# Waiting for the output's landing on TensorE instead of SyncE in a decode kernel

## The chip, the cores and the metric

The kernel runs on one core of a Trainium2 chip. The metric is device time in microseconds of one execution of the program; lower is better. The time quoted for a kernel is a median over several executions. A profile of one further execution goes with it; its own time is stated beside its span, because the span is only the time from the first to the last instruction of the kernel and the execution's time is a little longer.

## The reference

A decode step for four sequences (B = 4, one new token each, D = 576). Two branches read the same normalised input and are added to the residual:

```python
x = A_x
xn = _layernorm(x)
return x + A(xn) + B(xn)

# A: attention over a cache
q = (x @ wq).reshape(4, 1, 32, 128)          # 32 query heads, 16 kv heads
k, v = last 2048 rows of k_cache, v_cache    # each 4 x 16 x 2048 x 128 bf16
o = softmax(q k^T * 128**-0.5) v
return o.reshape(4, 1, 4096) @ wo            # wo: 4096 x 576

# B: an MLP pair with a shift in time
h  = gelu(layernorm(x) @ w1)                 # 576 x 576
x1 = x + shift(h) @ w2                       # 576 x 576
return x1 + gelu(layernorm(x1) @ w3) @ w4    # 576 x 4608, 4608 x 576
```

Nearly all bytes are the keys and values: 2 x 33.6 MB in bf16. The output is 4 x 576 values in bf16, 4.6 KB.

## The kernel before

The program is written as lists of operations, one list for each engine (`prog["pe"]`, `"pe2"`, `"pe3"`, `"dve"`, `"act"`, `"pool"`, `"sp"`). `add` appends an operation with the events it waits for, the event it signals and a key; `add_dma` does so for a DMA (its issue is L199). Each list is sorted by key and then written out by `emit_program`, which puts the waits ahead of the operation (L640). The order of an engine's work is therefore the order of the keys. TensorE's three lists are written with two loops between them: `pe`, then the loop over the keys, then `pe2`, then the loop over the values, then `pe3`.

The stages, in order of time:

- The small first part: layer norms on VectorE and ScalarE, the products with wq, w1, w2 and w3 on TensorE (lists `pe`).
- Keys: 16 chunks of 2 MB are loaded into a ring of 4 slots by DMAs that SyncE issues. TensorE transposes each chunk block by block (L485), VectorE and ScalarE move the blocks from PSUM to SBUF (L469, L468), TensorE forms the scores (L492).
- Softmax, and a transposition of the probabilities by matmuls (L514, list `pe2`).
- Values: 8 chunks of 4 MB through 4 slots. VectorE spreads the probabilities over heads (L545), TensorE multiplies (L553).
- The end (list `pe3`): the attention output is folded and transposed, then h2 @ w4 and o @ wo are accumulated into the same two PSUM tiles, `ACC[0]` and `ACC[1]` (one for each half of the 576 columns; both by L392). wo comes in five pieces of 13, 10, 5, 3 and 1 of its 32 rows for a partition, so that TensorE has little left to do when the last piece lands. ScalarE copies one half to `out_sb` (L608), VectorE the other (L609), and ScalarE issues the DMA of `out_sb` to the output (its key is 10000, the last of its list).

SyncE's list holds all loads except x, in the order of their keys, each behind the event that frees its slot. Its last operation, with key 10001, is a bare wait: it holds SyncE until the semaphore of the output's DMA has its full count (L301). Nothing stands behind it in SyncE's list. The events "PV..." that release the last loads are those of the values' products, so SyncE has issued its last load long before the end.

The last operations of `pe3` are the products with the last piece of wo, written for h = 1 and then for h = 0 with the events `AOl1` and `AOl0`, which L609 and L608 wait for.

Of the kernel before, what the change touches and what calls it, by code (L numbers as in the profile page):

```python
# [37 lines left out]
def bass_parallel_sum__sliding_block_cached__mixer_s_mlp__decode_kernel(  # L38
# [31 lines left out]
    with ExitStack() as ctx:  # L70
# [100 lines left out]
        S = {}  # L171
# [16 lines left out]
        def add(engine, emit, waits=(), sig=None, key=0.0, inc=None):  # L188
            seqc[0] += 1
            prog[engine].append(Op(emit, waits, sig, key, seqc[0], inc))  # L190

        def add_dma(pairs, skey, waits=(), key=0.0, engine="sp"):
            if skey not in S:
                S[skey] = sem("s_" + "_".join(str(k) for k in (skey if isinstance(skey, tuple) else (skey,))))
            dma_count[skey] = dma_count.get(skey, 0) + 16 * len(pairs)

            def emit(e):
                for o_, i_ in pairs:
                    e.dma_start(o_, i_).then_inc(S[skey], 16)  # L199
            add(engine, emit, waits, None, key)  # L200
            return ("dma", skey, dma_count[skey])
# [96 lines left out]
            a += rc  # L298
        assert a == 32
        ev_o = add_dma([(o2, out_sb[:])], "out", ["fin1", "fin0"], 10000, engine="act")  # L300
        add("sp", lambda e: e.wait_ge(S[ev_o[1]], ev_o[2]), (), None, 10001)  # L301


        def ln_ops(idx, src, dst, first_waits, tag, k0):
# [346 lines left out]
        e = nc.tensor  # L651
# [66 lines left out]
```

## Time and profile before

| | |
|---|---|
| median of three executions | 214.03 us (213.77 to 214.03) |
| the profiled execution's own time | 213.93 us |
| its span, first to last instruction | 212.6 us |
| TensorE busy with matmuls | 172.5 us (81%) |
| VectorE busy | 111.9 us (53%) |
| ScalarE busy | 58.6 us (28%) |
| read from HBM | 88.49 MB, 416 GB/s over the span |
| mean granted clock of TensorE | 0.928 |

In the profile PE is TensorE (PEld its weight loads), DVE is VectorE, ACT is ScalarE, POOL is GpSimd and SP is SyncE. A q behind the name stands for the engine's sequencer, which does the waiting and issues the DMAs: "SPq L301" is an instruction of SyncE's sequencer from line 301. Waits of this kind are not counted as busy time.

A view of the profile prints what lies in the span. The trace itself also records the updates of all semaphores, each with its time, for some microseconds ahead of the span and behind it, where the runtime's own instructions run. These records are used below; they are quoted as a plain list, with times in us counted from the start of the span, as in all views.

### The profile page before, as it was taken

The numbers are of one execution on the slowest core, as the hardware profiler recorded it, in microseconds if no ns is written. First come the engines' busy times: TensorE is split into PE (matmuls) and PEld (weight loads), VectorE is DVE, ScalarE is ACT, GpSimd is POOL, SyncE is SP. The second block draws the span as 40 slices with busy tenths as digits, with TensorE's granted clock in tenths as the row PEclk, the third lists the DMA queues.
The fourth block names the chain that finished last, engine by engine and source line by source line (L and its number), as shares of the span: only waits on it lengthen the run. The fifth ranks groups of instructions, "written<-read, shape, count | busy, mean of one in ns | idle before, by whom it ended". The sixth has DMA issues, their size and how long they took to land.

```text
span 212.6 us, 4856 instructions
## 1 busy us (share of the span) xinstructions
PE 172.5 (81%) x2212; PEld 133.7 (63%) x2216; DVE 111.9 (53%) x168; ACT 58.6 (28%) x69; POOL 15.6 (7%) x38
## 2 busy tenths in 40 slices
PE   1456147999999999999996089999989598997495
PEld 0222014888878888887774048988868487883262
DVE  5433200477776777777764869995575444003000
ACT  2004001366665566666656520000000000000000
POOL 8991000000000000000000000000000000000000
PEclk9997855899999999999999589999999889999799
DMA  6999999999999999999999999999999999999993
GB/s 242 453 444 445 429 396 416 432 425 427 429 416 438 432 422 429 435 422 424 432 444 438 444 407 459 413 425 453 407 444 438 419 425 410 451 476 393 407 408 131
DMA packets 5066, 88.65 MB, mean 417 GB/s; under 512 B 568, under 2 KB 704, under 8 KB 1216
## 3 DMA queue, kind: packets, MB, share of 16 engines
q1 hardware_dynamic: 5040, 88.49, 97.7%
q8 instruction: 8, 0.13, 0.3%
q14 instruction: 2, 0.02, 0.0%
q10 hardware_dynamic: 16, 0.01, 0.0%
HBM read 88.49 MB, written 0.00 MB: 416 GB/s over the span
## 4 chain that ended last, share of the span: by engine, by line
DMA 47%; PE 45%; DVE 4%; SPq 1%; ACT 1%; issue 1%
PE ps L485 23%; DMA vring<-in_A_wo_dram 15%; DMA vring<-in_B_w_dram 13%; DMA vring<-in_A_v_cache_dram 12%; PE ps L553 11%; DMA kring<-in_A_k_cache_dram 7%; PE ps L492 6%; PE ps L430 2%; SPq L199 1%; DVE vring L520 1%; DVE rmax L498 1%; DVE ktb L545 1%; PE ps L514 1%; PE ps L347 1%; ACT ktb L468 0%
## 5 line engine op out<-in xcount | busy, mean ns | idle before, releaser
L469 DVE COPY ktb<-ps 128x1024 bf16<-128x1024 bf16 x80 | 53.8, 689 | 23.5 <-PE ps L485 23.4
L485 PEld LDWEIGHTS ps<-perm_bf,kring 128*128 128x128 bf16 x1024 | 58.2, 98 | 8.3 <-issue 7.6
L485 PE MATMUL ps<-perm_bf,kring 128*128 128x128 bf16 x1024 | 61.7, 220 | 0.2
L468 ACT ACTIVATE ktb<-ps 128x1024 bf16<-128x1024 bf16 x48 | 48.0, 1023 | 32.5 <-PE ps L485 32.1
L545 DVE TENSOR_TENSOR ktb<-kring,mH_bf 128x4096 bf16<-128x4096 bf16 x16 | 36.2, 2286 | 14.6 <-PE ps L553 14.6
L553 PE MATMUL ps<-vring,ktb 128*128 128x256 bf16 x256 | 30.3, 282 | 4.3 <-DMA vring<-in_A_v_cache_dram 3.5
L553 PEld LDWEIGHTS ps<-vring,ktb 128*128 128x128 bf16 x256 | 25.7, 101 | 8.5 <-issue 3.6
L553 PE MATMUL ps<-kring,ktb 128*128 128x256 bf16 x256 | 28.6, 273 | 0.9 <-DMA kring<-in_A_v_cache_dram 0.9
L553 PEld LDWEIGHTS ps<-kring,ktb 128*128 128x128 bf16 x256 | 25.0, 98 | 4.5 <-issue 1.1
L608 ACT ACTIVATE out_sb<-ps 4x288 bf16<-4x288 f32 x1 | 0.4, 399 | 84.6 <-PE ps L392 84.6
L492 PE MATMUL ps<-ktb,Qs 128*32 128x512 bf16 x272 | 17.8, 382 | 1.2 <-ACT ktb L468 1.2
L430 PE MATMUL ps<-vring,xs 128*8 128x320 bf16 (+1 forms) x72 | 4.5, 429 | 7.6 <-DMA vring<-in_B_w_dram 7.6
L492 PEld LDWEIGHTS ps<-ktb,Qs 128*32 128x32 bf16 x272 | 5.7, 96 | 6.7 <-DVE ktb L469 1.4
L514 PE MATMUL ps<-vring,pick_bf 128*32 128x256 bf16 x64 | 3.9, 411 | 6.4 <-DVE rinv L532 6.4
L609 DVE CAST out_sb<-ps 4x288 bf16<-4x288 f32 x1 | 0.4, 449 | 15.7 <-PE ps L392 15.7
L392 PE MATMUL ps<-vring,h2T_sb 128*4 128x288 bf16 x72 | 6.2, 347 | 3.1 <-DMA vring<-in_B_w_dram 3.1
L571 DVE TENSOR_SCALAR tmp<-ps,maskd 128x128 f32<-128x128 f32 x2 | 0.7, 350 | 14.8 <-PE ps L553 14.8
L430 PEld LDWEIGHTS ps<-vring,xs 128*8 128x8 bf16 x72 | 2.1, 110 | 9.8 <-DMA vring<-in_B_w_dram 8.0
L330 PE MATMUL ps<-ident_bf,xp_bf 4*128 4x4 bf16 x15 | 0.8, 163 | 8.1 <-DVE xp_bf L314 5.0
L392 PEld LDWEIGHTS ps<-vring,h2T_sb 128*4 128x4 bf16 x72 | 3.7, 101 | 5.8 <-DMA vring<-in_B_w_dram 3.6
L514 PEld LDWEIGHTS ps<-vring,pick_bf 128*32 128x32 bf16 x64 | 2.0, 118 | 8.2 <-DVE rinv L532 6.9
L239 POOL MEMSET ktb<- 128x8192 bf16 x1 | 6.9, 6924 | 0.0
(93 smaller groups left out, 78.6 us busy)
## 6 DMA issues: line engine op xcount, KB each, us to landing
kring<-in_A_k_cache_dram SPq DMA_DIRECT2D x16, 2048.0 KB, 13.8
vring<-in_A_v_cache_dram SPq DMA_DIRECT2D x4, 4096.0 KB, 24.6
kring<-in_A_v_cache_dram SPq DMA_DIRECT2D x3, 4096.0 KB, 34.0
vring<-in_B_w_dram SPq DMA_DIRECT2D x2, 5184.0 KB, 25.1
kring<-in_A_wq_dram SPq DMA_DIRECT2D x1, 4608.0 KB, 15.7
kring<-in_A_v_cache_dram SPq DMA_DIRECT2D x2, 2048.0 KB, 27.4
vring<-in_A_wo_dram SPq DMA_DIRECT2D x1, 1872.0 KB, 26.9
vring<-in_A_wo_dram SPq DMA_DIRECT2D x1, 1440.0 KB, 29.8
```

Of the source, the lines that this page charges most:

```text
L199: e.dma_start(o_, i_).then_inc(S[skey], 16)
L239: P(lambda e: e.memset(ktb[:, NKT // 2 * 1024:NKT * 1024], 0.0), key=-92, inc=(("E", LB - 2), 1))
L347: ins = e.matmul(ps[:, w, :], lhsT=zeros_bf[:, 0:128], rhs=zeros_bf[:, :], start=True, stop=True)
L392: return e.matmul(ACC[h], lhsT=lhsT, rhs=rhs, start=start, stop=stop, tile_position=(0, 32 * h), skip_group_check=True)
L430: ins = e.matmul(H2ps[k][32 * j:32 * j + 2 * B].rearrange("b (p t) -> b p t", t=n), lhsT=x_at(2, s_), rhs=w[:, :, 9 * j + t0:9 * j + t0 + ...
L468: return "act", lambda e: e.activation(out=ktbuf[:, n % NKT], in_=tb[n % 4], func=ACTF.Copy)
L469: return "dve", lambda e: e.tensor_copy(out=ktbuf[:, n % NKT], in_=tb[n % 4])
L485: ins = e.transpose(tb[j % 4][:, t, :], kslot_t(k)[:, 8 * kb + t, :], perm_bf[:])
L492: ins = e.matmul(Sps[32 * u:32 * u + 32, q, :].rearrange("p (t i) -> p t i", t=16), lhsT=Qs[:, k, 32 * u:32 * u + 32], rhs=ktgrp[:, (4 * k ...
L514: ins = e.matmul(ps[32 * j:32 * j + 32, 4 + qt, 256 * ih:256 * (ih + 1)].rearrange("p (t a e) -> p t a e", a=NPAIR, e=2), lhsT=pick_bf[:, ...
L545: return lambda e: e.tensor_tensor(out=PTpad[:, n % 4], in0=PTv[:, qt, NH * h:NH * (h + 1), bp, :].unsqueeze(2).to_broadcast([128, NH, NX, ...
L553: ins = e.matmul(ps[:, 0, 0:256], lhsT=PTpad[:, 2 * (k % 2) + h, 2 * g:2 * g + 2].rearrange("p t h e -> p (t h e)"), rhs=vslot(k)[:, Dh * ...
```

## The change

The bare wait for the output's semaphore leaves SyncE's list and goes to the end of TensorE's last list, with the same semaphore, the same count and the same key:

```diff
         ev_o = add_dma([(o2, out_sb[:])], "out", ["fin1", "fin0"], 10000, engine="act")
-        add("sp", lambda e: e.wait_ge(S[ev_o[1]], ev_o[2]), (), None, 10001)
+        add("pe3", lambda e: e.wait_ge(S[ev_o[1]], ev_o[2]), (), None, 10001)
```

Key 10001 sorts behind all other keys of `pe3`, so the wait is TensorE's last operation, as it was SyncE's. The DMA that writes the output stays with ScalarE. SyncE's list now ends with the last load of wo.

## The prediction

> **What bounds the kernel now.** I read the views from the end of the span backwards, since the change touches only the end. First the page's chain of work and its DMA line.
>
> ```profile
> span 212.6 us, 4856 instructions
> ...
> DMA  6999999999999999999999999999999999999993
> ...
> DMA 47%; PE 45%; DVE 4%; SPq 1%; ACT 1%; issue 1%
> ```
>
> The DMA engines are full in all slices but the first and the last. The stages up to the last piece of wo are set by loads and by TensorE; the change touches neither. Next the chain of waits in order of time over the last stretch, and the timeline of it.
>
> ```profile
> 178.35 31.68 DMA vring<-in_A_wo_dram
> 210.03 0.04 issue
> 210.07 0.70 PE ps L392 x8
> 210.78 0.44 DVE out_sb L609
> ```
>
> ```profile
> 210.07 0.66 PE L392 MATMUL ps<-vring,ORT 128*4 128x288 bf16 x8 [0.30 <-DMA vring<-in_A_wo_dram]
> 210.76 0.45 DVE L609 CAST out_sb<-ps 4x288 bf16<-4x288 f32 x1 [15.72 <-PE ps L392]
> 210.80 0.40 ACT L608 ACTIVATE out_sb<-ps 4x288 bf16<-4x288 f32 x1 [84.57 <-PE ps L392]
> 211.28 0.28 ACTq L199 DMA_DIRECT2D out_dram<-out_sb  x1
> ```
>
> The reader is to see a strict sequence: wo lands, eight matmuls to 210.73, two copies to 211.21, one DMA issued at 211.28. TensorE has no work after 210.73. Then the wait itself, in the view of its line and in SyncE's waits.
>
> ```profile
> L301 SPq EVENT_SEMAPHORE  x1: 17/17/17, 212.6 to 212.6; - x1
> ...
> 176.92 2.33 SPq L199 DMA_DIRECT2D vring<-in_A_wo_dram  x5
> ...
> SPq L301 <- DMA out_dram<-out_sb: 33.3, 1, 33.3
> ```
>
> The first row is the last instruction of the span: SyncE's wait takes 17 ns once its semaphore is there, at 212.6. SyncE issued its last load by 176.92 + 2.33 = 179.25 and then sat for 33.3 us. Both engines are idle when the output lands, so inside the span only the reaction of one idle sequencer is exchanged for that of another.
>
> The execution took 213.93 us, its span 212.6: **1.3 us lie outside the span**, and there the engine that waits last may matter. No view prints that stretch, but the trace's records of semaphore updates do. The list leaves out the kernel's own semaphores, except number 168, the output's:
>
> ```
> 168 (output):       211.731 212.423 212.455 212.503 212.556
> 2, ahead of span:    -0.370  -0.336  -0.297  -0.253  -0.230  -0.118  -0.080  -0.046   0.001
> 2, end, round 1:    210.938 211.916 211.955 211.998 212.717 212.761 212.799 212.833 212.880
> 2, end, round 2:    213.759 213.793 213.831 213.876 213.899 213.997 214.036 214.070 214.116
> resets 207 to 255:  212.834 ... 212.923
> resets 156 to 206:  212.906 ... 213.214
> resets 105 to 155:  212.951 ... 213.230
> resets  54 to 104:  212.931 ... 213.164
> resets   7 to  53:  213.191 ... 213.535
> ```
>
> Semaphore 2 is counted up nine times in each round: it is a barrier of the five engines, there and back. Round 1 tells the order. The first update, at 210.938, comes before VectorE and ScalarE have finished (211.21), before SyncE has, and right after TensorE's last matmul; GpSimd has been idle since the start. So the first is TensorE's. The second, third and fourth come from 211.916 on, after ScalarE issued its DMA. The fifth, at 212.717, follows the landing at 212.556 and SyncE's wait: it is SyncE's, and the other four come back at once, 44, 38, 34 and 47 ns apart. **TensorE is first on the way out and last on the way back; SyncE is the turning point.** Then every engine resets about fifty semaphores. The block that starts latest, at 213.191, is the one whose engine was let go last: TensorE's. Round 2 starts at 213.759, with TensorE again. The end of the execution hangs on TensorE's release at 212.880.
>
> **The change part by part.** What it removes: SyncE's wait. SyncE then arrives at the barrier soon after 179.25, and waits there. From the landing to TensorE's release the path now is 212.556 to 212.717 (reaction, the wait, SyncE's steps up to its update: 0.161) and 212.717 to 212.880 (back: 0.163), together **0.324 us**.
>
> What it adds: one waiting instruction at the end of TensorE's stream. Nothing of the kernel is queued behind it; TensorE's arrival at the barrier is, and all four other engines wait for that. TensorE's bare waits in this trace are in the views of lines 683, 666 and 640:
>
> ```profile
> L683 PEldq EVENT_SEMAPHORE  x8: 51/51/51, 133.0 to 187.1; - x8
> ...
> L666 PEldq EVENT_SEMAPHORE  x16: 51/51/51, 38.2 to 110.2; - x16
> ...
> L640 ACTq EVENT_SEMAPHORE  x17: 17/17/17, 16.0 to 211.2; - x17
> L640 PEldq EVENT_SEMAPHORE  x14: 51/51/6997, 5.0 to 204.1; - x14
> ```
>
> A wait costs TensorE's sequencer 51 ns where the others take 17. Against the records of the semaphores, 38 of these waits start 28 or 29 ns after the update they waited for; SyncE's started 16 ns after the last update of 168 (212.556 to 212.572). So the terms of the new path are:
>
> - Reaction: 0.028. The wait: 0.051. Both from rows of the same kind of instruction on the same engine.
> - From the end of the wait to TensorE's update of semaphore 2. The trace doesn't show this case. From below: SyncE took 212.589 to 212.717, 0.128. From above: the view of line 703 has TensorE's first instruction of the kernel at 0.32 us, and its last barrier update stood at 0.001, which is 0.319 for a stretch of runtime instructions.
>
> ```profile
> L703 SPq DRAIN  x1: 7/7/7, 0.0 to 0.0; - x1
> ...
> L703 PEldq DRAIN  x1: 8/8/8, 0.3 to 0.3; - x1
> ```
>
>   Between them stand two cases of exactly "TensorE ends, then updates semaphore 2": the last matmul's signal at 210.776 to 210.938, 0.162, and its last reset at 213.535 to 213.759, 0.224. I take 0.224, the one in which the sequencer alone is at work, as after a wait. A gain below zero is excluded: an update can't come before the wait ends.
> - Around the barrier: with TensorE last, all eight steps are still ahead, with the other four engines already standing in it. The trace shows that case twice: -0.370 to 0.001 is 0.371, and 213.759 to 214.116 is 0.357. I take 0.364.
>
> Sum: 0.028 + 0.051 + 0.224 + 0.364 = 0.667, less 0.324: **+0.34 us**. With the low ends: 0.028 + 0.051 + 0.128 + 0.357 = 0.564, so +0.24. With the high ones: 0.028 + 0.051 + 0.319 + 0.371 = 0.769, so +0.45. From TensorE's release on, resets and round 2 go as before, shifted. The span itself should end at 212.556 + 0.028 + 0.051 = 212.635, 0.05 later than now.
>
> The page "Runtime: NRT & Kernel Launch" of the Trainium skill, section "The ~15µs preamble/postamble breakdown", describes a serpentine through the five engines of about 355 ns in eight hops of 44 ns; the rounds of 0.357 and 0.371 here agree. By hops alone, four more of them would be some 0.18 us, an estimate from that page.
>
> What else changes: all code of TensorE ahead of the wait stays at its place, since the wait is the last operation. SyncE's stream is one instruction shorter and ends at 179.25 instead of 212.6; nothing that it does afterwards shows in the records before the barrier lets it go. The 33.3 us that it no longer waits are worth nothing. The DMA that carries the output is issued by ScalarE after the same two copies.
>
> The sum stands against the profiled execution: 213.93 + 0.34 = **214.27 us**. The median shown, 214.03, is 0.10 above that execution, and the three times spread over 0.26. 0.2% is 0.43 us, about what a measurement of this kernel can tell from no change; the forecast is a loss, but a smaller one.
>
> **The rivals.**
>
> 1. *The tail costs more than the two thirds of a microsecond summed* (slower). TensorE takes its code in blocks, and fetches are in the page's table of queues:
>
> ```profile
> q8 instruction: 8, 0.13, 0.3%
> ```
>
>   Eight fetches of 16 KB; by the trace's DMA records each takes 0.95 to 1.25 us, the last from 208.236 to 209.488. If one more instruction pushes TensorE's closing instructions over the end of a block that has not been fetched, TensorE stands for one fetch at the very end, where nothing covers it: +0.34 + 1.0 to 1.25, 215.3 to 215.5. One 64-byte instruction in 16 KB makes this unlikely, and the fetch at 208.2 ran ahead of need. The same side is reached when TensorE's step from wait to update is as slow as the 0.319 case and somewhat more: +0.45 to +0.6, 214.4 to 214.5. It decides beyond 0.31 us for that step, where the sum passes +0.43. For it: TensorE is the slowest sequencer in each row above (51 against 17 ns, DRAIN at 0.3 against 0.0).
>
> 2. *The time is not taken behind the barrier.* The updates go on to 214.116, and 212.589 + 1.34 = 213.93 is less than that, so the time's start or end can't be read off this list. If its end doesn't move with the barrier, only the reaction and the wait count: +0.05, 213.98. Against it: something of the order of the barrier's tail is in the 1.34 us.
>
> 3. *The barrier is a count and not a ring, and SyncE's steps come off the path* (faster). Then TensorE, the engine with the longest tail, goes on to its resets as soon as it has arrived itself: 0.028 + 0.051 + 0.162 to 0.224, plus the 0.311 that it took from 212.880 to 213.191, puts its first reset at 213.11 to 213.17 instead of 213.191, a gain of 0.02 to 0.08: 213.85 to 213.91. Against it: the even spacing of 34 to 47 ns on the way back, which is what a chain looks like. A gain beyond 0.43 us would need a reset phase that SyncE could do early; its block of resets, the first and shortest (0.089 us), isn't on the path now.
>
> 4. *Nothing happens*: the hops are paid but something else of the same size ends, or the wait is overlapped with the end of TensorE's queue: 213.93 to 214.1.
>
> **How the numbers follow.** The forecast (ring, +0.24 to +0.45) gets 0.58; rival 1 gets 0.19, most of it for the dearer step; rivals 2 and 4 together 0.15; rival 3 0.08. The likeliest time is 214.27. About a quarter of the forecast's own chance lies beyond +0.43 when the scatter of the medians is put on it, 0.14; with rival 1 that makes slower by over 0.2% 0.33. Faster by over 0.2% could come only from a tail that behaves unlike rival 3's price, or from scatter: 0.06. Within 0.2% is the rest, 0.61. For the range: 214.17 to 214.38 by the bounds of the sum; scatter of the size of the three times (0.26) and rivals 2 and 3 on the lower side give 213.75, scatter and the dearer step on the upper side 214.75. A stalled fetch (under 0.05) stays outside.
>
> **What would show it.** In the profile of the changed kernel the last instruction is TensorE's wait at line 301, with 51 ns, and the span is 212.6 as before, to 0.1 us but for what the loads scatter. SyncE's wait row is gone. In the updates of semaphore 2, the first four of round 1 no longer come before the landing: nine updates follow one another within 0.36 us, the first of them 0.2 to 0.4 us after the last update of 168. From the landing to the ninth update it is 0.56 to 0.77 instead of 0.324. The resets 7 to 53 are still the last. The prediction is wrong if the ninth update comes as soon after the landing as now (then TensorE's place in the barrier was misread), if a fetch shows after 211, or if the tail shifts by the sum and the time does not (rival 2).

## The result and the profile after

The changed kernel takes 214.26 us (median of 22 executions, 213.95 to 214.59) against 213.97 us before (22 executions, 213.64 to 214.26): a ratio of 1.0014, 95% interval 1.0008 to 1.002. That is +0.17 to +0.43 us, with +0.29 between the medians. The loss is small, but it is there.

The profiled execution of the changed kernel took 214.39 us. The two lines of its page that answer to those of before, its span and its DMA line:

```profile
span 212.8 us, 4860 instructions
...
DMA  6999989999999999999999999999999999999993
```

The DMA engines are as full as before. The last stretch, in the chain of waits in order of time (start, length, what) and then in the timeline:

```profile
176.86 33.33 DMA vring<-in_A_wo_dram
210.19 0.04 issue
210.24 0.70 PE ps L392 x8
210.94 0.44 DVE out_sb L609
```

```profile
210.24 0.66 PE L392 MATMUL ps<-vring,ORT 128*4 128x288 bf16 x8 [0.29 <-DMA vring<-in_A_wo_dram]
210.93 0.45 DVE L609 CAST out_sb<-ps 4x288 bf16<-4x288 f32 x1 [14.21 <-PE ps L392]
210.96 0.40 ACT L608 ACTIVATE out_sb<-ps 4x288 bf16<-4x288 f32 x1 [84.49 <-PE ps L392]
211.45 0.28 ACTq L199 DMA_DIRECT2D out_dram<-out_sb  x1
```

From the landing of wo on (210.19 against 210.03) it is the same sequence as before, with the same lengths, 0.16 to 0.17 us later. The last load of wo itself began 1.5 us earlier in the chain and took 1.65 us longer. The 0.16 us were there when it landed; they are scatter of the loads between two executions and not the change, for in a second trace of the changed kernel, e9_after_look below, the output landed at 212.532, earlier than the 212.556 of before. The next two views show what the change did: the wait in the view of line 301, and SyncE's waits.

```profile
L301 PEldq EVENT_SEMAPHORE  x1: 51/51/51, 212.7 to 212.7; - x1
...
SPq L199 <- PE ps L485: 83.7, 14, 18.3
SPq L199 <- PE ps L553: 57.4, 5, 20.4
SPq L199 <- PE ps L369: 18.2, 1, 18.2
SPq L703 <- PEq L703: 0.7, 1, 0.7
```

Line 301 now belongs to TensorE and takes 51 ns where SyncE took 17. SyncE's wait of 33.3 us has gone from the list, and the execution is none the shorter for it. Behind the span, the updates of the output's semaphore, of the barrier's semaphore 2 and the resets of TensorE's block:

```
168 (output):       211.894 212.587 212.622 212.672 212.715
2, end, round 1:    213.082 213.116 213.154 213.198 213.222 213.319 213.359 213.393 213.440
2, end, round 2:    214.223 214.257 214.296 214.340 214.363 214.462 214.500 214.534 214.581
resets   7 to  53:  213.651 ... 213.999
```

Before, four of the nine updates of round 1 stood ahead of the landing (168's last update) and five behind it. Now all nine stand behind it, in 0.358 us. From the landing to the ninth update, TensorE's release, it is 0.725 us instead of 0.324. From the landing to the end of round 2 it is 1.866 us instead of 1.560. The two profiled executions differ by 214.39 - 213.93 = 0.46 us: 0.16 from the landing (212.715 against 212.556), 0.31 from this tail.

### The profile page after: what moved, and what is told of

It is laid out like the page before. It is cut to its first block, busy times and chain, and to the rows that moved or that the text cites. A ratio compares the mean times of both kernels' runs of the same rounds, so it can differ in the third digit from the quotient of the medians.

```text
span 212.8 us, 4860 instructions
## 1 busy us (share of the span) xinstructions
PE 172.2 (81%) x2216; PEld 132.2 (62%) x2216; DVE 112.3 (53%) x168; ACT 59.3 (28%) x69; POOL 15.5 (7%) x38
## 4 chain that ended last, share of the span: by engine, by line
DMA 61%; PE 30%; DVE 4%; SPq 2%; ACT 1%; issue 1%
DMA kring<-in_A_k_cache_dram 21%; DMA vring<-in_A_wo_dram 16%; DMA vring<-in_B_w_dram 13%; PE ps L485 12%; DMA vring<-in_A_v_cache_dram 12%; PE ps L553 10%; PE ps L492 4%; PE ps L430 2%; SPq L199 2%; DVE vring L520 1%; DVE rmax L498 1%; DVE ktb L545 1%; PE ps L514 1%; PE ps L347 0%; ACT ktb L468 0%
## 5 line engine op out<-in xcount | busy, mean ns | idle before, releaser
L485 PEld LDWEIGHTS ps<-perm_bf,kring 128*128 128x128 bf16 x1024 | 57.4, 98 | 9.5 <-issue 7.4
L468 ACT ACTIVATE ktb<-ps 128x1024 bf16<-128x1024 bf16 x48 | 48.7, 1023 | 31.8 <-PE ps L485 31.0
L553 PE MATMUL ps<-kring,ktb 128*128 128x256 bf16 x256 | 30.1, 281 | 2.6 <-DMA kring<-in_A_v_cache_dram 2.6
L553 PE MATMUL ps<-vring,ktb 128*128 128x256 bf16 x256 | 28.6, 273 | 4.2 <-DMA vring<-in_A_v_cache_dram 3.4
L553 PEld LDWEIGHTS ps<-kring,ktb 128*128 128x128 bf16 x256 | 25.7, 101 | 6.9 <-issue 2.8
L553 PEld LDWEIGHTS ps<-vring,ktb 128*128 128x128 bf16 x256 | 24.8, 98 | 7.6 <-issue 3.5
L330 PEld LDWEIGHTS ps<-ident_bf,xp_bf 4*128 4x128 bf16 x15 | 0.6, 101 | 9.9 <-DVE xp_bf L314 5.4
L392 PE MATMUL ps<-vring,ORT 128*4 128x288 bf16 x64 | 4.6, 286 | 2.3 <-DMA vring<-in_A_wo_dram 2.3
```

The costliest lines, as they stand in the source:

```text
L392: return e.matmul(ACC[h], lhsT=lhsT, rhs=rhs, start=start, stop=stop, tile_position=(0, 32 * h), skip_group_check=True)
L468: return "act", lambda e: e.activation(out=ktbuf[:, n % NKT], in_=tb[n % 4], func=ACTF.Copy)
L485: ins = e.transpose(tb[j % 4][:, t, :], kslot_t(k)[:, 8 * kb + t, :], perm_bf[:])
L553: ins = e.matmul(ps[:, 0, 0:256], lhsT=PTpad[:, 2 * (k % 2) + h, 2 * g:2 * g + 2].rearrange("p t h e -> p (t h e)"), rhs=vslot(k)[:, Dh * ...
```

## The experiments

Two theories stood at the start. **A, the place in the barrier:** the loss is the steps of the barrier that are still ahead when the last engine arrives. **B, the slow sequencer:** the loss is TensorE's own time between the landing and its arrival. The prediction's sum had a part of each. Further theories, C to I, stand in the expectations of the runs that were made for them. For every run the trace gives the parts of the tail, all in us from the landing; "arrival" is the first update of semaphore 2 by the engine that waited, "release" the ninth update, "to reset" what TensorE took from its release to its first reset.

| kernel | who waits | wait ends | arrival | release | to reset | end of round 2 |
|---|---|---|---|---|---|---|
| before | SyncE | 0.033 | 0.161 | 0.324 | 0.311 | 1.560 |
| e8_before_look | SyncE | 0.033 | 0.161 | 0.324 | 0.220 | 1.473 |
| e4_pe_busy | SyncE | 0.034 | 0.161 | 0.324 | 0.220 | 1.472 |
| e7_pe_fin | SyncE | 0.034 | 0.161 | 0.324 | 0.217 | 1.465 |
| changed | TensorE | 0.079 | 0.367 | 0.725 | 0.211 | 1.866 |
| e9_after_look | TensorE | 0.079 | 0.271 | 0.629 | 0.212 | 1.770 |
| e10_after_look2 | TensorE | 0.079 | 0.270 | 0.629 | 0.305 | 1.856 |
| e5_both | both | 0.079 | 0.271 | 0.627 | 0.210 | 1.766 |
| e6_pe_more | TensorE | 0.034 | 0.221 | 0.578 | 0.212 | 1.719 |
| e11_pe_incs | TensorE | 0.534 | 0.861 | 1.219 | 0.211 | 2.359 |
| e1_act | ScalarE | 0.038 | 0.146 | 0.471 | 0.218 | 1.617 |
| e2_pool | GpSimd | 0.041 | 0.583 | 0.869 | 0.217 | 2.015 |
| e3_dve | VectorE | 0.049 | 0.195 | 0.436 | 0.215 | 1.580 |

Each row is one trace. In e5_both "wait ends" and "arrival" are TensorE's. Which update belongs to which engine shows in the traces of the last three rows: with ScalarE waiting, one update of round 1 stands ahead of the landing, with GpSimd two, with VectorE three, so the order on the way out is TensorE, ScalarE, GpSimd, VectorE, SyncE. The other stretches of the tail hardly vary: TensorE's resets take 0.341 to 0.348, from the last of them to round 2 it is 0.224 or 0.225, round 2 takes 0.357 or 0.358.

**The wait on the three other engines.** The edit is the engine's name:

```diff
-        add("sp", lambda e: e.wait_ge(S[ev_o[1]], ev_o[2]), (), None, 10001)
+        add("act", lambda e: e.wait_ge(S[ev_o[1]], ev_o[2]), (), None, 10001)
```

and in the same way `"pool"` and `"dve"`.

> The wait moved to ScalarE. Theory A (place in the barrier): what counts is how many steps of the barrier are still ahead when the last engine arrives. From ScalarE's update to TensorE's release it was 0.324 us in the changed kernel (213.116 to 213.440); with a reaction and wait of 0.04 and SyncE's 0.13 for the step to the barrier, landing to TensorE's release is 0.49 us, against 0.324 with SyncE waiting: the end of the second round moves by +0.17 us. Rival B (TensorE's own slow sequencer makes the whole loss, the place nothing): landing to release 0.32 to 0.35, end +0.00 to +0.03. Time by A 214.14, by B 213.98.

> The wait moved to GpSimd. A: 0.286 us of steps remain (213.154 to 213.440 in the changed kernel), so landing to TensorE's release is 0.04 + 0.13 + 0.29 = 0.46 us, end +0.13. B: +0.00 to +0.03. Time by A 214.10, by B 213.98.

> The wait moved to VectorE, the engine next to SyncE in the barrier. A: 0.242 us of steps remain (213.198 to 213.440), landing to TensorE's release 0.05 + 0.13 + 0.24 = 0.42 us, end +0.10. B: +0.00 to +0.03. Time by A 214.07, by B 213.98.

Against 213.93 us before (33 executions on that chip): ScalarE 214.08 us, ratio 1.0005 (0.9996 to 1.0015); GpSimd 214.39, 1.0022 (1.0013 to 1.0031); VectorE 214.04, 1.0004 (0.9995 to 1.0013). The views of line 301 of the three:

```profile
L301 ACTq EVENT_SEMAPHORE  x1: 17/17/17, 212.5 to 212.5; - x1
```

```profile
L301 POOLq EVENT_SEMAPHORE  x1: 17/17/17, 212.5 to 212.5; - x1
```

```profile
L301 DVEq EVENT_SEMAPHORE  x1: 21/21/21, 212.6 to 212.6; - x1
```

No wait is as long as TensorE's, and yet none of the three kernels has SyncE's 0.324 us to the release: 0.471 for ScalarE and 0.436 for VectorE, where A had 0.49 and 0.42 and B 0.32 to 0.35. B alone falls. The times of these two agree with A but can't be told from no change, so this rests on one trace of each. GpSimd's 0.869 is neither theory's number. From its arrival to the release it is 0.286, just A's steps; but from the end of its wait to its arrival it took 0.542 us, where SyncE takes 0.128, ScalarE 0.108, VectorE 0.146 and TensorE 0.19 (0.288 in the profile above; the runs below show which is usual). So the engine's own step to the barrier counts too, and it isn't TensorE that has the dearest. GpSimd's +0.46 us in the medians (interval +0.28 to +0.66, which leaves out A's +0.13) is the largest loss of the five places. What GpSimd does in its step isn't shown.

**TensorE kept at work.** Seven matmuls on zeros behind the last product, with the wait on SyncE:

```diff
+        add("pe3", pe_idle(7), key=10000)
```

> SyncE waits for the output as before; TensorE runs seven more matmuls on zeros after its last product (they change no output), so that it gets to the barrier about 212.2 to 212.4, shortly before the landing, and not 1.9 us before its release. It asks why TensorE's way from its release to its first reset was 0.211 us in the changed kernel and 0.311 before. Theory C (it depends on how long TensorE has stood idle in the barrier): about 0.21, end 0.10 earlier, 213.87. Rival D (it depends on TensorE being the last to arrive): 0.31 as before, 213.97.

The time was 213.88 us against 213.93, ratio 0.9999 (0.999 to 1.0008). The timeline has the seven matmuls from 210.71 to 212.39, on past the issue of the output's DMA at 211.34:

```profile
210.71 1.68 PE L564 MATMUL ps<-zeros_bf 128*128 128x512 bf16 x7
210.82 0.45 DVE L610 CAST out_sb<-ps 4x288 bf16<-4x288 f32 x1 [15.69 <-PE ps L392]
210.85 0.40 ACT L609 ACTIVATE out_sb<-ps 4x288 bf16<-4x288 f32 x1 [84.53 <-PE ps L392]
211.34 0.28 ACTq L199 DMA_DIRECT2D out_dram<-out_sb  x1
```

TensorE's first update came at 212.548, 0.05 us ahead of the landing, and the release stayed 0.324 us behind it. So an arrival 0.05 us ahead of the landing, and not 1.6 us ahead as before, cost nothing here. From release to reset it was 0.220, as C had it, and D, which had 0.31 for this run, is wrong. But in e1_act, e2_pool and e3_dve TensorE had stood in the barrier since 210.9 or 211.0 and took 0.215 to 0.218 as well, so C is wrong too.

**The added half alone.** SyncE keeps its wait and TensorE gets one:

```diff
         add("sp", lambda e: e.wait_ge(S[ev_o[1]], ev_o[2]), (), None, 10001)
+        add("pe3", lambda e: e.wait_ge(S[ev_o[1]], ev_o[2]), (), None, 10001)
```

> The added half of the change alone: TensorE waits for the output, and SyncE waits for it too, as before. Theory A (place in the barrier): TensorE is first in the order, all others wait for its update, so SyncE's wait has ended long before the barrier comes to it; landing to TensorE's release 0.72 us as in the changed kernel (0.725), time as there, 214.26. Rival E (part of the cost or of a gain comes from SyncE's stream ending early): landing to release differs from 0.725 by over 0.02, and the time moves by as much.

The time was 214.22 us against 213.92, ratio 1.0013 (1.0004 to 1.0022), that of the changed kernel. Both waits stand at the end of this kernel, line 301 and line 302:

```profile
L301 SPq EVENT_SEMAPHORE  x1: 17/17/17, 212.7 to 212.7; - x1
```

```profile
L302 PEldq EVENT_SEMAPHORE  x1: 51/51/51, 212.7 to 212.7; - x1
```

The added half is the whole loss; taking SyncE's wait away gives nothing that these runs can tell from zero. The release came 0.627 us behind the landing and not 0.725, by which E would hold; the further traces of the changed kernel show that 0.63 is what it has too.

**More instructions behind the wait, first try.** Four more bare waits behind TensorE's:

```diff
+        for k in ("act", "dve", "pool", "FO"):
+            add("pe3", lambda e, k=k: e.wait_ge(S[k], 1), (), None, 10002)
```

> The changed kernel with four more bare waits behind TensorE's wait, on semaphores that have long had the value. Theory B (TensorE's own slow sequencer is a part of the cost): its instructions stood 0.106 to 0.110 us apart where a bare wait followed a bare wait; joined in pairs the five waits make three instructions, two more than in the changed kernel, so wait to update grows from 0.288 to about 0.50 and the time by 0.21, 214.47; one instruction for each wait would make it +0.43. Rival A alone (only the place counts): 0.288 plus next to nothing, 214.26.

It was 214.15 us against 213.92, ratio 1.0008 (0.9999 to 1.0017), and the tail was shorter than the changed kernel's. The view of the waits' line shows why the test was no test:

```profile
L303 PEldq EVENT_SEMAPHORE  x3: 51/51/1951, 210.4 to 210.7; - x3
```

The five waits became three instructions, and the output's was joined to another as the last of them: it began at 210.659, lasted 1951 ns and ended 0.034 us behind the landing. Nothing stood behind it. Theory B was not tested by this run. It shows something else, in one trace: a wait of two semaphores that had already begun ended 0.034 us behind the landing, where the bare one ends at 0.079.

**More instructions, second try.** Four counts of a semaphore that nobody waits for:

```diff
+        for _ in range(4):
+            add("pe3", lambda e: e.sem_inc(S["FO"], 1), (), None, 10002)
```

> The changed kernel with four counts of a semaphore that nobody waits for behind TensorE's wait: instructions that can't be moved ahead of it. Theory B (each of TensorE's own instructions behind the landing is paid in full): three or four more instructions at 0.05 (their length) to 0.11 (their distance) each, landing to update of the barrier 0.27 + 0.15 to 0.44, time 214.4 to 214.7. Rival A alone (only the place in the barrier counts): as the changed kernel, 214.24.

The time was 214.66 us against 213.90, ratio 1.0036 (1.0024 to 1.0048), that is +0.51 to +1.03 us. The first count was joined to the wait; the four instructions are

```profile
L303 PEldq EVENT_SEMAPHORE  x4: 51/51/51, 212.6 to 213.0; - x4
```

by the trace 0.15 us apart, at 212.591, 212.745, 212.894 and 213.045. The last ended 0.534 us behind the landing and the arrival came another 0.327 later. Against e9_after_look the release moved by 0.590 us, from 0.629 to 1.219, and the end of round 2 by 0.589. Theory A alone falls: instructions of the waiting engine behind the landing are paid in full in the tail, and the interval of the times holds the 0.89 us by which this tail is longer than SyncE's in e8_before_look. Three additional instructions cost more than I had bounded (0.15 to 0.44), by their distance of 0.15 and by 0.135 in the step behind them; where the 0.135 come from isn't shown.

**The step to the barrier where nothing hangs on it.** SyncE waits for the output, TensorE for ScalarE's copy:

```diff
+        add("pe3", lambda e: e.wait_ge(S["act"], resolve("fin0")[1]), key=10000)
```

> SyncE waits for the output as before; TensorE has a bare wait on ScalarE's last copy at its end, which is over about 1.3 us before the landing. What the step from a bare wait to TensorE's update of the barrier costs, where nothing hangs on it: 0.288 as in the changed kernel if the bare wait itself makes TensorE slow, 0.16 as behind the last matmul before if not. The time is that of the kernel before, 213.97, by both.

One execution, 213.87 us.

```profile
L608 PEldq EVENT_SEMAPHORE  x1: 51/51/51, 211.3 to 211.3; - x1
```

The wait ended at 211.318 and TensorE's update came at 211.510: 0.192 us. That is neither 0.288 nor 0.16. The bare wait costs TensorE's step a little against a matmul's end (0.162), and the 0.288 of the changed kernel's profile isn't its usual value.

**The two kernels once more, for their traces.** No edit.

> The kernel before once more, for its trace. In its profile TensorE took 0.311 us from its release to its first reset and in five other traces 0.211 to 0.220; only in that one did the granted clock go to a half between the two. Theory F (the clock made the 0.311): with the clock at full there, 0.21 to 0.22, and the end of the second round 1.46 us after the landing. Rival G (it belongs to the kernel before): 0.31 and 1.56 us.

> The changed kernel once more, for its trace. TensorE's step from the end of its wait to its update of the barrier was 0.288 us in its profile, 0.192 in two others that have a bare wait at the same place (with SyncE waiting too, and on ScalarE's copy). Theory H (the 0.288 was a stall of that one execution): 0.19, landing to release 0.63, landing to the end of the second round 1.77 us. Rival I (it belongs to the changed kernel): 0.29, 0.72 and 1.87.

> The same a third time, since one look can't tell a stall of one execution from a rule. H: 0.19, 0.63 and 1.77 us. I: 0.29, 0.72 and 1.87.

The kernel before took 213.75 us and 0.220 from release to reset: rival G falls. The changed kernel took 214.12 and 214.41 us; the step from wait to arrival was 0.192 and 0.191 in both, so H holds and I falls. In the second of the two the 0.305 from release to reset came back, now in the changed kernel. So there is **a stall of 0.09 to 0.1 us that hits TensorE's sequencer in some executions at some place**: from release to reset in the profile of before and in e10_after_look2, from wait to arrival in the profile of the changed kernel. Theory F, the clock, isn't borne out. In the profile of before the granted clock went to a half at 212.986, inside the longer stretch, but in the other two traces it stayed at full through theirs. In e6_pe_more and e7_pe_fin it fell while TensorE stood in the barrier, and from release to reset TensorE took the usual 0.212 and 0.217 at half the clock. In e11_pe_incs the clock fell at 212.950, between two counts that stood 0.151 apart like the others. What makes the stall stays open.

Without it the tails are 1.465 to 1.473 us with the wait on SyncE (three traces) and 1.766 to 1.770 with the wait on TensorE (e5_both, e9_after_look): **+0.30 us**, which is the +0.29 of the medians.

## Why the prediction was right

The forecast was +0.34 us with +0.24 to +0.45 for the sum; measured was +0.29, with +0.30 in the tails. The mechanism is the one forecast. That the time forecast, 214.27, stands 0.01 us from the median, 214.26, is luck: the sum was 0.04 above the tails' +0.30, and the execution that it was added to, 213.93, is 0.04 below the median before, 213.97. By its steps, with e8_before_look and e9_after_look for the two kernels:

- *Path taken away: 0.324.* Measured 0.324 in four traces.
- *Reaction and wait: 0.028 + 0.051.* Measured 0.079. (The 38 waits behind the 0.028 are not those of the three lines named there alone: by the trace of before 23 stand on lines 640, 666 and 683, the others on 660, 670, 681 and 703. The size is the same on all.)
- *From the wait to TensorE's update: 0.224, between 0.128 and 0.319.* Measured 0.192 (0.288 in the profile with the stall). This is the term that was too large by 0.03 and nearly all of the sum's error. The neighbour that I chose, the step behind the last reset, was no nearer than the one behind the last matmul, 0.162; the value lies between them.
- *Around the barrier: 0.364, between 0.357 and 0.371.* Measured 0.358.
- *From the release on as before, shifted.* Right without the stall (0.220 and 0.212 to the reset), but the single profile of before had 0.311 there, and I had taken it as TensorE's usual step. It stood on both sides of the sum and so did no harm; a forecast of the tail's absolute length would have been 0.09 off.
- *The span ends 0.05 later against the landing.* 0.079 against 0.033.

Of the rivals, the dearer tail did not come: the step was 0.192, not beyond 0.31, and in the changed kernel's trace the last of the eight fetches in queue 8 began at 208.398, by the DMA records, with none behind it. The ground given for it, that TensorE is the slowest sequencer, holds for the bare waits (51 ns) but not for the step to the barrier, where GpSimd took 0.542. "The time isn't taken behind the barrier" is refuted: the executions' own times lie 0.18 to 0.19 us ahead of the end of round 2 in eleven traces, and 0.09 in e1_act and e2_pool, whatever the tail's length (1.465 to 2.359). (The difference of 0.1 us in these two has the size of the stall; whether it is one, no record shows.) "A count and not a ring" is refuted by the order: with TensorE, ScalarE, GpSimd or VectorE last, what remains to the release is 0.358, 0.325, 0.286 and 0.241, shorter with each place nearer to SyncE. "Nothing happens" is refuted by the interval.

The page "Runtime: NRT & Kernel Launch" of the Trainium skill, section "The ~15µs preamble/postamble breakdown", gives the serpentine through the five engines, in its row on the barrier ahead of the kernel, as eight hops of 44 ns, some 355 ns in all. The whole of 0.358 behind this kernel agrees with it.

The steps of the barrier aren't equal in the trace: in the changed kernel they are 0.034, 0.038, 0.044, 0.024 up to SyncE, then 0.097 from SyncE to the next, then 0.040, 0.034, 0.047. With SyncE last that long one is 0.044 (212.717 to 212.761). So by the traces moving the wait from SyncE to TensorE costs 0.195 us of steps around the barrier (0.358 - 0.163), and the other 0.11 are TensorE's own: 0.271 to its arrival against SyncE's 0.161, that is 0.012 in the reaction, 0.034 in the wait and 0.064 in the step behind it. Both theories hold a part, two thirds A and one third B. The prediction's estimate of 0.18 from the figure of the Trainium skill lies a little below the 0.195.

## What to carry to other kernels

The span of the profile isn't the end of the execution: behind it all engines go through a barrier and reset semaphores, and the engine that waits last for the output decides how much of the barrier is left. In this program the place for that wait is SyncE, the turning point of the barrier; everywhere else it cost 0.11 us (VectorE, 1.580 against 1.473) to 0.54 us (GpSimd, 2.015) of tail, through the steps left and through the engine's own way to the barrier. Both of these tails are from one trace each; in the times of the executions the losses with TensorE and GpSimd are clear of the noise, those with VectorE and ScalarE are not. A change of a tenth of a per cent is not read from one profile against another, since two executions of one kernel differ by as much; the lengths between the landing and the barrier's updates repeat to a few ns in most traces and show it.

## What the runs showed of the hardware

- GpSimd took 0.542 us from the end of a bare wait to its update of the barrier, in one trace (e2_pool); ScalarE 0.108, SyncE 0.128, VectorE 0.146, TensorE 0.192 where it wasn't stalled.
- TensorE's counts of a semaphore stood 0.15 us apart behind a wait, though each is listed with 51 ns (e11_pe_incs).
- A stall of 0.09 to 0.1 us in TensorE's steps outside the span, in three of the thirteen traces (the profiles of before and of the changed kernel, and e10_after_look2), at no fixed place.
